# Gate products of a banded-attention and two-MLP kernel: which banks they alternate between, and what may stand before a bank's reading in the engines' lists

## The chip, the cores and the metric

The kernel runs on one core of a Trainium2 chip. The metric is device microseconds of one execution on that core. TensorE (PE) does the matmuls and has its own row for weight loads (PEld); VectorE (DVE), ScalarE (ACT) and GpSimd (POOL) do the elementwise work, and SyncE (SP) issues the DMAs.

## The reference

The part that matters, cut:

```
x = attention(q, k, v)            # 4 batches, 8 heads, 768 rows, 64 wide: 4 sinks and a window of 128 rows
a = x @ w1                        # (3072 x 512) @ (512 x 1024)
b = x @ w2
h = a * b @ w3                    # (a * b) @ w3
x = h @ w_out
h = x @ w_in                      # the second MLP
solu = h * softmax(h)
out = layernorm(solu) * g_ln @ w_out
```

All of it is fp32. The change lies in the two products a and b and in their elementwise product a * b, the gate.

## The kernel before

The kernel does its matmuls in a split form: an fp32 operand is held as a high part and a low part, each in a shortened fp32 type, and a product is three matmuls (high by high, high by low, low by high). The large products are also done by seven products on blocks of half the size in place of eight (Strassen and Winograd's scheme; `FACTORS` says which sum of blocks each of the seven takes on the left and on the right). So every operand is a sum of blocks, and each sum is made and split into parts by **operand pieces**: sums (`plus`, L368, on DVE or POOL), high parts (`acopy`, L158, on ACT) and low parts (`do_step`, L365, on DVE). New weights are first converted by L342, L351 (DVE), L359 (POOL) and L158 (ACT).

The program goes through attention, then the gate, then the product by w3 with w_out folded into it, then the second MLP. The gate, which is what the change touches, works on one batch (768 rows of x) after the other, and for each batch on four column groups m: 16 groups in all. A group has seven products k, each for two halves z (z = 0 for x @ w1, z = 1 for x @ w2). One (k, z) is six matmuls of 128x384 (`product`, which calls `mm` on L155), so there are 224 of them. They are written into PSUM, which the program holds as four tiles of two banks each: in the trace and below, bank0 is a tile with the banks X of z = 0 and Y of z = 0, bank1 has Z of z = 0 and X of z = 1, bank2 has Y of z = 1 and Z of z = 1, and bank3 has the banks 6 and 7, which the gate doesn't use before the change. Product 2 goes to X, products 5 and 3 to Z, products 1, 6, 7 and 4 to Y. Products that go to the same bank one after the other without a restart add to what stands there.

A finished bank is **read**: by an ACT copy into scratch memory (`copy`, L158, arF<-bank), or by a DVE addition of the bank to what was copied before (`two`, L948, arF<-bank,arF). Before the change a group has copies of products 1, 6, 7 and 4 and DVE readings of the others and of the bank Z at product 7; two finished halves are then multiplied on DVE (`two` with ALU.mult, arF<-arF), and the result is sent to DRAM by a DMA (`send`, L938).

What follows what on each engine isn't the order in which the code is written. Every step is put on a list of tasks (`op`) with an engine, an own estimate of its duration and a rank; `arrange` runs a small simulation of the engines over the list, in which an engine that comes free takes the task of the lowest rank among those whose inputs are ready. The instructions are then issued in that order, and each engine works through its own list strictly in order on the chip. Operand pieces of the next group or batch, conversions of new weights and readings of banks share the lists of DVE and ACT.

Of the kernel before, what the change touches and what calls it, by code (L numbers as in the profile page):

```python
# [26 lines left out]
    mask=62.62, load=22.12, scores=-355.79, max=-67.26, exp=-12.34, total=-62.48, norm=40.89, T=-21.59,  # L27
    stay=29.46, R_T=-100.61, sink_T=-182.3, T_copy=-50.24, sink_copy=-116.03, V=51.95, out=-62.87, w_load=18.71,
    w_a=-69.73, w_b=67.42, w_c=24.26, w_hi=47.52, w_lo=3.94, fold=163.21, fold_out=40.78, parts=-92.47,
    spill=-105.5, x_parts=71.86, later=-5.34, stage=0.0,  # L30
)
WO_AT, WO_BY, W3_AT, W3_BY, W12_AT, W12_BY = -4.0, 3.0, 21.0, 3.4, 30.0, 12.0
OWN_NS, OTHER_NS, PE_NS = 19, 232, 400

OVER = dict(DVE=82, ACT=95, POOL=45)

PART_OF = dict(scores="rows", V="columns")
SWITCH = {("all", "rows"): 95, ("all", "columns"): 95, ("columns", "all"): 100, ("columns", "rows"): 100}
# [10 lines left out]
def arrange(tasks, ranks=None):  # L49
# [3 lines left out]
    rank = [t[2] + ranks[t[3]] for t in tasks]  # L53
# [18 lines left out]
    free = {e: 0 for e in engine}  # L72
# [3 lines left out]
    kind = "all"  # L76
# [7 lines left out]
    while len(order) < len(tasks):  # L84
        start, eng = min(
            (free[e] if go[e] else max(free[e], wait[e][0][0]), e) for e in free if go[e] or wait[e]
        )
        while wait[eng] and wait[eng][0][0] <= start:
            n = heapq.heappop(wait[eng])[1]
            heapq.heappush(go[eng], (rank[n], n))  # L90
        n = heapq.heappop(go[eng])[1]
        change = 0
        if eng == "PE":
            heapq.heappush(go[eng], (rank[n], n))
            to = {x: PART_OF.get(tasks[x[1]][3], "all") for x in go[eng]}
            x = min(go[eng], key=lambda x: (x[0] + stay * ((kind, to[x]) in SWITCH), x[1]))
            go[eng].remove(x)
            heapq.heapify(go[eng])
            n, change, kind = x[1], SWITCH.get((kind, to[x]), 0), to[x]
        if tasks[n][0][-1] == "+" and port > start:  # L100
            others = [x for x in go[eng] if tasks[x[1]][0][-1] != "+"]
            if others:
                heapq.heappush(go[eng], (rank[n], n))
                go[eng].remove(min(others))
                heapq.heapify(go[eng])
                n = min(others)[1]
            else:
                start = port
        order.append(n)
        end = start + tasks[n][1] + change  # L110
        free[eng] = max(start, end - OVER.get(eng, 0))
        if tasks[n][0][-1] == "+":
            port = free[eng]
        for m in follow[n]:
            lag = OWN_NS if engine[m] == eng else PE_NS if eng == "PE" else OTHER_NS
            at_ns[m] = max(at_ns[m], end + tasks[n][8] + lag)
            before[m] -= 1
            if not before[m]:
                heapq.heappush(wait[engine[m]], (at_ns[m], m))
# [4 lines left out]
def attention_moe_kernel(  # L124
# [52 lines left out]
    def path(stack, banded):  # L177
# [744 lines left out]

        tasks = []

        def op(eng, ns, rank, outs, ins, f, *args, after=0, both=False, then=None):

            r = set().union(*(toks(a) for a in ins)) if ins else set()
            w = set().union(*(toks(a) for a in outs))
            if then is not None:
                r.add(then)  # L930
            tasks.append((eng + "+" * (eng == "POOL" or both), ns, rank, "stage", f, args, r - w, w, after))

        def dma(rank, out, in_, then=None):

# [5 lines left out]
        def copy(rank, out, in_, cols, eng="ACT"):  # L940
            if eng == "ACT":
                op("ACT", ns_of("ACT", cols), rank, [out], [in_], acopy, out, in_)
            else:
                op("DVE", ns_of("DVE", cols), rank, [out], [in_], lambda: DVE.tensor_copy(out=out, in_=in_))
# [26 lines left out]
        X, Y, Z = 0, 1, 2  # L971
        BANK = {1: Y, 6: Y, 7: Y, 4: Y, 2: X, 5: Z, 3: Z}

        def product(k, z, rank, ns, width, left, right):

            b = bank[3 * z + BANK[k]][:, 0:width]
            (lh, ll), (rh, rl) = left, right
            items = []
            for c in range(len(lh)):
                items += [(lh[c], rh[c]), (lh[c], rl[c]), (ll[c], rh[c])]  # L980
            op("PE", ns, rank, [b], [*lh, *ll, *rh, *rl], run, b, items, k in (1, 2, 5))
            return b

        both = [(1, 0), (1, 1), (2, 0), (6, 0), (2, 1), (6, 1), (5, 0), (7, 0), (5, 1), (7, 1), (4, 0), (3, 0), (4, 1), (3, 1)]
        when = {}
        for i, (k, z) in enumerate(both):
            when.setdefault(k, i)
# [40 lines left out]
        for bi, b in enumerate(order):  # L1028
# [4 lines left out]
            for m in range(4):  # L1033
# [33 lines left out]
                for k, z in both:  # L1067
                    l, r = FACTORS[k]
                    bk = product(
                        k, z, now, MM, TH, [[gw[z][:, l, u, c, :] for c in range(2)] for u in range(2)],  # L1070
                        [[xop[:, xlie[r], u, c, :] for c in range(2)] for u in range(2)],
                    )
                    now += MM
                    if k in (1, 6, 7):
                        copy(now, {1: p_, 6: u2, 7: u3}[k][z], bk, TH)
                    if k == 2:
                        two("DVE", now + 2000, p_[z], bk, p_[z], TH)
                        if z:
                            two("DVE", now + 5000, p_[0], p_[0], p_[1], TH, ALU.mult)
                            send(0, p_[0], now + 5000)  # L1080
                    if k == 7:
                        two("DVE", now, u3[z], bank[3 * z + Z][:, 0:TH], u3[z], TH)
                        if z:
                            two("DVE", now + 5000, u3[0], u3[0], u3[1], TH, ALU.mult)
                            send(3, u3[0], now + 5000)
# [10 lines left out]
                            send(2, u2[0], now + 5000)  # L1096


        MM = 2082
        abop = [hold[:, 12 * i * KB:12 * (i + 1) * KB].rearrange("p (u c n) -> p u c n", u=2, c=4) for i in range(3)]  # L1100
        abk = [t.rearrange("p (c n) -> p c n", c=4) for t in (
# [317 lines left out]
```

## Time and profile before

| | us |
|---|---|
| median of three runs (926.5 to 927.68) | 927.65 |
| the profiled execution, its own time | 927.59 |
| its span | 925.2 |
| PE busy, of the span | 888.6 (96%) |
| DVE busy | 700.0 (76%) |
| ACT busy | 548.8 (59%) |
| the gate, from its first matmul to the first of the next stage | 263.38 to 521.68 |

A row of the trace that lists single instructions gives the start, the duration, the engine, the line, what is written and read, how many instructions of the same kind follow one another (x), and in brackets how long the engine was idle before and what released it. "PE ... [0.74 <-DVE arF L948]" is a matmul that stood still for 0.74 us until a DVE addition on line 948 was done. Durations of one instruction include a start-up that overlaps the one before, so that the distance between starts (the pitch) can be shorter than the duration.

### The profile page before, as it was taken

The page shows a single profiled execution, that of the slowest core. Times are in us where ns is not written, and L with a number is a line of the kernel's source. Part 1 is how long each engine was busy: PE and PEld are TensorE (multiplying, and loading weights), DVE is VectorE, ACT ScalarE, POOL GpSimd, SP SyncE. Part 2 cuts the span into 40 slices and gives each one's busy share as a digit, 9 for nine tenths or more (in the row PEclk, how much of TensorE's full clock was granted, in tenths as well). Part 3 has the DMA queues.
Part 4 walks back from the last instruction along what each step waited for, and adds up shares of the span by engine and source line. Part 5 has one row for each costly group of instructions (what it writes and reads, how often), then busy time and mean ns, then how long its engine had stood idle before and what let it go on. Part 6 is the DMA issues. An engine that isn't in the chain of part 4 may idle for free.

```text
span 925.2 us, 15584 instructions
## 1 busy us (share of the span) xinstructions
PE 888.6 (96%) x5392; PEld 749.8 (81%) x5392; DVE 700.0 (76%) x1646; ACT 548.8 (59%) x1251; POOL 183.4 (20%) x243
## 2 busy tenths in 40 slices
PE   7999999999999899999998999999999999999996
PEld 3555665665579898989888999999888888999996
DVE  6988888676958786773776897794788877898761
ACT  6887877765746444752543566563667576755441
POOL 2664655451225322120000000000010011000000
PEclk9999999999999999999999999999999999999999
DMA  7566657632236367563132265443243343454411
GB/s 273 182 232 235 204 188 252 215 123 80 69 100 184 128 203 240 191 214 125 56 130 76 85 208 188 158 146 124 104 146 127 125 160 137 172 194 143 177 58 61
DMA packets 84760, 143.72 MB, mean 155 GB/s; under 512 B 6976, under 2 KB 58432, under 8 KB 82240
## 3 DMA queue, kind: packets, MB, share of 16 engines
q1 hardware_dynamic: 84672, 142.64, 46.1%
q8 instruction: 44, 0.72, 0.3%
q14 instruction: 44, 0.36, 0.1%
HBM read 95.43 MB, written 47.19 MB: 154 GB/s over the span
## 4 chain that ended last, share of the span: by engine, by line
PE 82%; DVE 12%; DMA 2%; issue 2%; ACT 1%; POOL 1%; SPq 0%; DVEq 0%; ACTq 0%; POOLq 0%
PE bank L155 56%; PE s L155 11%; PE pa L155 6%; PE pat L644 4%; DVE arF L948 3%; PE bank L1233 2%; DVE hold L365 2%; DVE g L365 2%; PE pn L656 1%; PE pn L650 1%; DVE ar L368 1%; DVE sa L600 1%; DMA arF<-in_moe_w_in_dram 1%; DVE ring L661 1%; DMA qk<-in_qk_dram 1%
## 5 line engine op out<-in xcount | busy, mean ns | idle before, releaser
L155 PE MATMUL bank<-hold,g 128*128 128x384 f32 x2016 | 360.7, 338 | 15.4 <-DVE arF L948 11.1
L155 PEld LDWEIGHTS bank<-hold,g 128*128 128x128 f32 x2016 | 349.8, 189 | 26.4 <-DVE arF L948 19.2
L155 PE MATMUL bank<-g,hold 128*128 128x512 f32 (+1 forms) x1080 | 202.2, 342 | 0.6 <-ACT ar L158 0.5
L155 PEld LDWEIGHTS bank<-g,hold 128*128 128x128 f32 x1080 | 169.2, 190 | 22.3 <-ACT ar L158 1.0
L158 ACT ACTIVATE arF<-bank 128x384 f32<-128x384 f32 (+1 forms) x160 | 80.8, 519 | 115.5 <-PE bank L155 80.5
L615 ACT ACTIVATE sa<-sa,st 128x288 f32<-128x288 f32 (+1 forms) x192 | 95.7, 501 | 20.3 <-DVE st L600 17.4
L600 DVE CUSTOM_DVE_ANT_0 sa<-s,masks 128x288 f32<-128x288 f32 (+1 forms) x192 | 76.8, 418 | 23.9 <-PE s L155 23.6
L948 DVE TENSOR_TENSOR arF<-bank,arF 128x384 f32<-128x384 f32 x96 | 53.0, 554 | 51.7 <-PE bank L155 23.4
L365 DVE TENSOR_TENSOR hold<-ar,hold 128x384 fp32r<-128x384 f32 (+2 forms) x137 | 84.6, 648 | 8.5 <-ACT hold L158 8.2
L1221 POOL TENSOR_TENSOR stt<-stt,half 128x1 f32<-128x1 f32 x24 | 17.3, 721 | 371.0 <-DVE stt L1219 363.2
L158 ACT ACTIVATE hold<-ar 128x384 fp32r<-128x384 f32 (+2 forms) x137 | 75.4, 586 | 18.0 <-DVE ar L368 13.8
L155 PE MATMUL s<-qk 64*128 64x288 f32 (+2 forms) x384 | 75.0, 439 | 8.0 <-DMA qk<-in_qk_dram 6.0
L158 ACT ACTIVATE ar<-bank 128x256 f32<-128x256 f32 (+1 forms) x80 | 33.8, 423 | 73.9 <-PE bank L155 73.5
L155 PE MATMUL bank<-g,g 128*128 128x256 f32 x504 | 66.3, 285 | 3.9 <-DVE ar L948 2.2
L661 DVE COPY ring<-pat 128x512 f32<-128x512 f32 (+1 forms) x96 | 60.9, 640 | 11.3 <-PE pat L644 10.9
L155 PEld LDWEIGHTS bank<-g,g 128*128 128x128 f32 x504 | 62.5, 192 | 5.5 <-DVE ar L948 3.0
L155 PEld LDWEIGHTS s<-qk 64*128 64x128 f32 x384 | 34.0, 193 | 35.9 <-issue 15.0
L155 PE MATMUL s<-hold 128*128 128x512 f32 x192 | 59.5, 423 | 0.0
L155 PE MATMUL pa<-ring,vn 128*64 128x256 f32 (+1 forms) x448 | 56.1, 357 | 1.5 <-DVE ring L661 1.0
L644 PE MATMUL pat<-identr,sa 128*128 128x128 f32 x352 | 56.5, 281 | 0.0
L948 DVE TENSOR_TENSOR ar<-bank,ar 128x256 f32<-128x256 f32 (+1 forms) x60 | 28.4, 475 | 32.9 <-ACT ar L158 19.1
L368 DVE TENSOR_TENSOR ar<-ar 128x256 f32<-128x256 f32 (+3 forms) x92 | 51.5, 571 | 0.8
(97 smaller groups left out, 1150.4 us busy)
## 6 DMA issues: line engine op xcount, KB each, us to landing
qk<-in_qk_dram SPq DMA_DIRECT2D x15, 1088.0 KB, 5.1
raw<-in_moe_w_dram SPq DMA_DIRECT2D x24, 512.0 KB, 5.1
abd<-arF SPq DMA_DIRECT2D x64, 192.0 KB, 2.0
lnd<-arF SPq DMA_DIRECT2D x48, 256.0 KB, 2.2
ar<-lnd SPq DMA_DIRECT2D x8, 1024.0 KB, 5.6
vn<-in_v_dram SPq DMA_DIRECT2D x16, 384.0 KB, 3.2
arF<-abd SPq DMA_DIRECT2D x8, 768.0 KB, 5.0
ar<-abd SPq DMA_DIRECT2D x8, 768.0 KB, 4.7
```

The costliest lines, as they stand in the source:

```text
L155: PE.matmul(o, lhsT=l, rhs=r, start=start, stop=stop, skip_group_check=True)
L158: ACT.activation(out=o, in_=i, func=AF.Copy, scale=s)
L365: eng.tensor_tensor(out=lo, in0=src, in1=fl(hi), op=ALU.subtract)
L368: eng.tensor_tensor(out=out, in0=a, in1=b, op=ALU.add if sign > 0 else ALU.subtract)
L600: DVE.tensor_tensor_reduce(out=sa[s][:, h, :n], in0=s_bank[s_at(s, h)][:, :n], in1=m_qb[j, h], op0=ALU.add, op1=ALU.min, scale=-scale, sca ...
L615: ACT.activation(out=a[:, h, :n], in_=a[:, h, :n], func=AF.Exp, scale=-1.0, bias=st_t[s][:, h:h + 1], accum_out=rs_t[p, j // 2][:, i:i + 1],)
L644: PE.transpose(pt[:, h, u, :], a[:, h, o:o + P], ident)
L650: PE.transpose(pn[0:n + 2 * SINKS, s % 2, :], a[:, 256 - n:256 + 2 * SINKS], ident)
L661: DVE.tensor_copy(out=ring[:, :, 2 * j + u0:2 * j + 2, :], in_=pat_t.pop(s)[:, :, u0:, :])
L948: eng, ns_of(eng, cols), rank, [out], [a, b], lambda: engines[eng].tensor_tensor(out=out, in0=a, in1=b, op=o),
L1221: op("POOL", 550, rank + 900, [st[7]], [st[6]], lambda: POOL.tensor_tensor(out=st[7], in0=st[6], in1=half, op=ALU.pow))
L1233: PE.transpose(bk[:, i * P:(i + 1) * P], e[:, (4 * g + i) * P:(4 * g + i + 1) * P], ident)
```

## The change

Four edits. The products of a group are put in the order 1, 2, 6, 5, 7, 3, 4, with both halves of each one after the other. In the odd groups (m = 1 and 3) the products that went to the banks Y go to the banks 6 and 7 of the tile bank3. Product 5 is copied by ACT in place of product 7, and DVE then adds the bank of product 7 to that copy. And `arrange` gets a rule for the gate: an operand piece on ACT or DVE (kind "gate") that would end later than 200 ns before the next reading of a bank (kind "bank") that is known to come due on that engine isn't placed; another piece that fits is taken, or the engine is left idle until the reading is due.

```
+MARGIN = 200
...
+        if tasks[n][3] == "gate" and eng in ("DVE", "ACT"):
+
+            due = min((t for t, m in wait[eng] if tasks[m][3] == "bank" and rank[m] < rank[n] + 4000), default=None)
+            if due is not None:
+                fits = [x for x in [(rank[n], n)] + sorted(go[eng]) if start + tasks[x[1]][1] - OVER[eng] + MARGIN <= due]
+                if not fits:
+                    heapq.heappush(go[eng], (rank[n], n))
+                    free[eng] = due
+                    continue
...
-            tasks.append((eng + "+" * (eng == "POOL" or both), ns, rank, "stage", f, args, r - w, w, after))
+            kind = "stage"
+            if gate_is_on[0] and eng in ("ACT", "DVE"):
+                kind = "bank" if {a.tensor.name for a in ins} & banks else "gate"
+            tasks.append((eng + "+" * (eng == "POOL" or both), ns, rank, kind, f, args, r - w, w, after))
...
-            b = bank[3 * z + BANK[k]][:, 0:width]
+            b = bank[6 + z if other and BANK[k] == Y else 3 * z + BANK[k]][:, 0:width]
...
-        both = [(1, 0), (1, 1), (2, 0), (6, 0), (2, 1), (6, 1), (5, 0), (7, 0), (5, 1), (7, 1), (4, 0), (3, 0), (4, 1), (3, 1)]
+        both = [(k, z) for k in (1, 2, 6, 5, 7, 3, 4) for z in range(2)]
...
-                        [[xop[:, xlie[r], u, c, :] for c in range(2)] for u in range(2)],
+                        [[xop[:, xlie[r], u, c, :] for c in range(2)] for u in range(2)], m % 2 == 1,
...
-                    if k in (1, 6, 7):
-                        copy(now, {1: p_, 6: u2, 7: u3}[k][z], bk, TH)
+                    if k in (1, 6, 5):
+                        copy(now, {1: p_, 6: u2, 5: u3}[k][z], bk, TH)
...
-                        two("DVE", now, u3[z], bank[3 * z + Z][:, 0:TH], u3[z], TH)
+                        two("DVE", now, u3[z], bk, u3[z], TH)
...
+        gate_is_on[0] = False
```

The lists before the gate are the same as before, and so are those from the w3 stage on. Three places show what moves in the gate; the four tiles have the numbers bank0_3009 to bank3_3012.

**PE, the last group of the gate (the fourth batch, m = 3).** Each x6 is one (k, z); x12 is two of them after each other into the same tile. hold and g23 are the operands. Before:

```order
L155 MATMUL bank0_3009<-hold_74,g23_3003 128x384 x6
L155 MATMUL bank2_3011<-hold_74,g23_3003 128x384 x6
L155 MATMUL bank0_3009<-hold_74,g23_3003 128x384 x12
L155 MATMUL bank1_3010<-hold_74,g23_3003 128x384 x6
L155 MATMUL bank2_3011<-hold_74,g23_3003 128x384 x6
L155 MATMUL bank1_3010<-hold_74,g23_3003 128x384 x6
L155 MATMUL bank0_3009<-hold_74,g23_3003 128x384 x6
L155 MATMUL bank2_3011<-hold_74,g23_3003 128x384 x12
L155 MATMUL bank0_3009<-hold_74,g23_3003 128x384 x6
L155 MATMUL bank1_3010<-hold_74,g23_3003 128x384 x6
L155 MATMUL bank2_3011<-hold_74,g23_3003 128x384 x12
```

Now:

```order
L170 MATMUL bank3_3012<-hold_74,g23_3003 128x384 x12
L170 MATMUL bank0_3009<-hold_74,g23_3003 128x384 x6
L170 MATMUL bank1_3010<-hold_74,g23_3003 128x384 x6
L170 MATMUL bank3_3012<-hold_74,g23_3003 128x384 x12
L170 MATMUL bank1_3010<-hold_74,g23_3003 128x384 x6
L170 MATMUL bank2_3011<-hold_74,g23_3003 128x384 x6
L170 MATMUL bank3_3012<-hold_74,g23_3003 128x384 x12
L170 MATMUL bank1_3010<-hold_74,g23_3003 128x384 x6
L170 MATMUL bank2_3011<-hold_74,g23_3003 128x384 x6
L170 MATMUL bank3_3012<-hold_74,g23_3003 128x384 x12
```

Before, a tile came up again after one (k, z) into another tile, or at once. Now the two halves of products 1, 6, 7 and 4 go to the two banks of one tile back to back, and two of other products lie between. In the even groups (not shown) the tiles bank0, bank2 and bank1 take turns, with one (k, z) between two that go to the same tile at six places of each group.

**DVE, the fourth batch, m = 1 and the start of m = 2.** L948 (L968 now) with a bank is a reading, with arF alone the product of two halves; L368 (L383 now) are sums and L365 (L380 now) low parts of operands, that is pieces. Before:

```order
L948 TENSOR_TENSOR arF_3004<-arF_3004,bank2_3011 128x384
L368 TENSOR_TENSOR ar1_75<-ar1_75 128x256
L365 TENSOR_TENSOR g01_73<-ar1_75,g01_73 128x256
L948 TENSOR_TENSOR arF_3004<-bank2_3011,arF_3004 128x384
L365 TENSOR_TENSOR g01_73<-ar1_75,g01_73 128x2x256
L948 TENSOR_TENSOR arF_3004<-arF_3004 128x384
L365 TENSOR_TENSOR g01_73<-ar1_75,g01_73 128x2x256
L368 TENSOR_TENSOR ar1_75<-ar1_75 128x256 x2
L948 TENSOR_TENSOR arF_3004<-bank0_3009,arF_3004 128x384
L365 TENSOR_TENSOR g01_73<-ar1_75,g01_73 128x2x256 x3
L948 TENSOR_TENSOR arF_3004<-bank1_3010,arF_3004 128x384
L368 TENSOR_TENSOR ar1_75<-ar1_75 128x256
```

Now:

```order
L968 TENSOR_TENSOR arF_3004<-bank3_3012,arF_3004 128x384
L383 TENSOR_TENSOR ar1_75<-ar1_75 128x256
L968 TENSOR_TENSOR arF_3004<-bank3_3012,arF_3004 128x384
L968 TENSOR_TENSOR arF_3004<-bank1_3010,arF_3004 128x384
L968 TENSOR_TENSOR arF_3004<-bank2_3011,arF_3004 128x384
L968 TENSOR_TENSOR arF_3004<-arF_3004 128x384 x2
L968 TENSOR_TENSOR arF_3004<-arF_3004,bank3_3012 128x384
L380 TENSOR_TENSOR g01_73<-ar1_75,g01_73 128x2x256 x4
L968 TENSOR_TENSOR arF_3004<-bank0_3009,arF_3004 128x384
L380 TENSOR_TENSOR g01_73<-ar1_75,g01_73 128x256
L968 TENSOR_TENSOR arF_3004<-bank1_3010,arF_3004 128x384
L380 TENSOR_TENSOR g01_73<-ar1_75,g01_73 128x2x256
```

Before, one to three pieces stood right ahead of most readings. Now readings stand behind readings, and the pieces are gathered behind the last reading of a group, or single between readings that are further apart.

**DVE, the first batch, the fourth group (m = 3), where the weights g23 of this group are still being made.** Before, from the reading of product 7 to the low parts:

```order
L948 TENSOR_TENSOR arF_3004<-bank2_3011,arF_3004 128x384
L948 TENSOR_TENSOR arF_3004<-bank1_3010,arF_3004 128x384
L948 TENSOR_TENSOR arF_3004<-arF_3004 128x384
L948 TENSOR_TENSOR arF_3004<-arF_3004,bank2_3011 128x384
L948 TENSOR_TENSOR arF_3004<-bank0_3009,arF_3004 128x384
L948 TENSOR_TENSOR arF_3004<-bank2_3011,arF_3004 128x384
L365 TENSOR_TENSOR g23_3003<-ar1_75,g23_3003 128x2x256
L948 TENSOR_TENSOR arF_3004<-arF_3004 128x384
L365 TENSOR_TENSOR g23_3003<-arF_3004,g23_3003 128x2x256 x2
```

Now:

```order
L968 TENSOR_TENSOR arF_3004<-bank1_3010,arF_3004 128x384
L968 TENSOR_TENSOR arF_3004<-bank2_3011,arF_3004 128x384 x2
L968 TENSOR_TENSOR arF_3004<-arF_3004 128x384
L968 TENSOR_TENSOR arF_3004<-arF_3004,bank2_3011 128x384
L968 TENSOR_TENSOR arF_3004<-arF_3004 128x384
L380 TENSOR_TENSOR g23_3003<-ar1_75,g23_3003 128x2x256 x2
L380 TENSOR_TENSOR g23_3003<-arF_3004,g23_3003 128x2x256 x2
L968 TENSOR_TENSOR arF_3004<-arF_3004 128x384
```

Before, the readings stood among the low parts. Now the readings of products 7, 3 and 4 of z = 1 and two multiplications (the second of them of the same halves) all stand ahead of four low parts; product 6 of z = 0 of the fourth group takes the second of these low parts with its third matmul.

## Rows read from the trace of the kernel before

**Rows 1.** The page: part 1 (busy us, share, instructions), one group of part 5 (mean ns).

```profile
PE 888.6 (96%) x5392; PEld 749.8 (81%) x5392; DVE 700.0 (76%) x1646; ACT 548.8 (59%) x1251; POOL 183.4 (20%) x243
...
L155 PE MATMUL bank<-hold,g 128*128 128x384 f32 x2016 | 360.7, 338 | 15.4 <-DVE arF L948 11.1
```

**Rows 2.** Windows of batches 1, 4, all: PE, PEld, DVE, ACT, POOL, PEclk, DMA, GB/s.

```profile
263.38:329.53 66.15, 62.64 (x336) 59.58 (x337) 51.04 (x85) 35.84 (x70) 25.49 (x25) 0.97 0.48 151
...
456.20:521.68 65.48, 60.40 (x338) 57.93 (x337) 47.19 (x96) 29.61 (x61) 0.00 (x0) 1.00 0.32 101
sum 258.30, PE 243.78 PEld 233.49 DVE 180.82 ACT 129.01 POOL 45.98; mean PE 60.95 PEld 58.37 DVE 45.21 ACT 32.25 POOL 11.49
```

**Rows 3.** Waits of PEld in the gate (262 to 523): total us, times, longest.

```profile
PEld bank L155 <- DVE arF L948: 19.2, 24, 1.5
PEld bank L155 <- ACT arF L158: 4.4, 6, 1.3
```

**Rows 4.** Timeline of PE behind the gate (532 to 560): one run of matmuls without a gap.

```profile
531.80 28.41 PE L155 MATMUL bank<-hold,g 128*128 128x384 f32 x163
```

**Rows 5.** Windows at the gate's start; the columns of rows 2.

```profile
263.40:265.20 1.80, 1.80 (x6) 1.80 (x7) 0.00 (x0) 0.00 (x0) 0.00 (x0) 0.58 0.37 90
265.20:267.20 2.00, 2.00 (x8) 2.00 (x8) 0.00 (x0) 0.49 (x1) 0.00 (x0) 0.52 1.00 345
```

**Rows 6.** Timeline of the fourth batch, m = 1: the DVE list of the second place above.

```profile
473.12 0.42 DVE L368 TENSOR_TENSOR ar<-ar 128x256 f32<-128x256 f32 x1
...
473.46 0.42 DVE L365 TENSOR_TENSOR g<-ar,g 128x256 fp32r<-128x256 f32 x1
...
473.79 0.55 DVE L948 TENSOR_TENSOR arF<-bank,arF 128x384 f32<-128x384 f32 x1
...
474.40 5.48 PE L155 MATMUL bank<-hold,g 128*128 128x384 f32 x30 [0.74 <-DVE arF L948]
...
478.37 1.89 DVE L365 TENSOR_TENSOR g<-ar,g 128x512 fp32r<-128x512 f32 x3
...
480.18 0.55 DVE L948 TENSOR_TENSOR arF<-bank,arF 128x384 f32<-128x384 f32 x1
...
480.78 1.66 PE L155 MATMUL bank<-hold,g 128*128 128x384 f32 x8 [0.91 <-DVE arF L948]
```

**Rows 7.** Timeline of the third batch: a DVE reading with no piece ahead of it.

```profile
414.00 4.50 PE L155 MATMUL bank<-hold,g 128*128 128x384 f32 x25
...
415.83 0.56 DVE L948 TENSOR_TENSOR arF<-bank,arF 128x384 f32<-128x384 f32 x1 [0.48 <-ACT arF L158]
```

**Rows 8.** Timeline of the first batch: an ACT reading with no piece ahead of it.

```profile
280.46 3.81 PE L155 MATMUL bank<-hold,g 128*128 128x384 f32 x21
...
281.52 0.49 ACT L158 ACTIVATE arF<-bank 128x384 f32<-128x384 f32 x1 [0.57 <-PE bank L155]
```

**Rows 9.** Groups by line and shape in the gate (263.4 to 521.8): busy us, mean ns.

```profile
L948 DVE TENSOR_TENSOR arF<-bank,arF 128x384 f32<-128x384 f32 x95 | 52.4, 554 | 51.7 <-PE bank L155 23.4 <-ACT arF L158 22.6 <-ACT hold L158 3.9
L948 DVE TENSOR_TENSOR arF<-arF 128x384 f32<-128x384 f32 x49 | 29.8, 608 | 0.7
...
L365 DVE TENSOR_TENSOR g<-ar,g 128x512 fp32r<-128x512 f32 x18 | 13.6, 776 | 1.3 <-ACT g L158 1.3
...
L158 ACT ACTIVATE arF<-bank 128x384 f32<-128x384 f32 x112 | 54.4, 488 | 99.6 <-PE bank L155 80.5 <-DVE arF L948 13.0 <-DVE arF L342 3.2
```

**Rows 10.** Timeline of the first batch, third group: a reading late behind a DMA.

```profile
302.39 0.49 ACT L158 ACTIVATE arF<-bank 128x384 f32<-128x384 f32 x1 [0.30 <-DMA abd<-arF]
...
302.93 1.38 PE L155 MATMUL bank<-hold,g 128*128 128x384 f32 x6 [0.92 <-ACT arF L158]
```

**Rows 11.** Timeline of the second batch: a conversion that waits for its load.

```profile
351.82 1.24 ACT L158 ACTIVATE arF<-arF 128x512 f32<-128x512 f32 x2 [1.72 <-DMA arF<-in_moe_w_in_dram]
...
354.70 2.38 PE L155 MATMUL bank<-hold,g 128*128 128x384 f32 x12 [0.95 <-ACT arF L158]
```

**Rows 12.** Window of 120 us right behind the gate; the columns of rows 2.

```profile
522.00:642.00 120.00, 120.00 (x688) 119.11 (x687) 97.93 (x200) 66.71 (x141) 0.00 (x0) 1.00 0.51 165
```

More of the change, by code (lines that the diff above doesn't have):

```diff
@@ L29 @@
     w_a=-69.73, w_b=67.42, w_c=24.26, w_hi=47.52, w_lo=3.94, fold=163.21, fold_out=40.78, parts=-92.47,
-    spill=-105.5, x_parts=71.86, later=-5.34, stage=0.0,
+    spill=-105.5, x_parts=71.86, gate=0.0, bank=0.0, later=-5.34, stage=0.0,
 )
@@ L99, in arrange @@
             n, change, kind = x[1], SWITCH.get((kind, to[x]), 0), to[x]
+        if tasks[n][3] == "gate" and eng in ("DVE", "ACT"):
[6 more added lines that the diff above has]
+                    continue
+                if fits[0][1] != n:
+                    heapq.heappush(go[eng], (rank[n], n))
+                    go[eng].remove(fits[0])
+                    heapq.heapify(go[eng])
+                    n = fits[0][1]
         if tasks[n][0][-1] == "+" and port > start:
@@ L923, in path @@
         tasks = []
+        gate_is_on = [True]
         def op(eng, ns, rank, outs, ins, f, *args, after=0, both=False, then=None):
@@ L972, in path, with product @@
         BANK = {1: Y, 6: Y, 7: Y, 4: Y, 2: X, 5: Z, 3: Z}
-        def product(k, z, rank, ns, width, left, right):
-            b = bank[3 * z + BANK[k]][:, 0:width]
+        def product(k, z, rank, ns, width, left, right, other=False):
+            b = bank[6 + z if other and BANK[k] == Y else 3 * z + BANK[k]][:, 0:width]
             (lh, ll), (rh, rl) = left, right
```

## The prediction

> **What bounds the kernel now.** I read the page's busy times first: PE is busy for 888.6 us of the span of 925.2 [rows 1], so the matmuls bound the kernel, and a change that leaves their number alone can win only what PE stands still. Behind the gate there is nothing of the kind to win: in the 120 us after it PE is busy for 120.00 us [rows 12]. I then cut the gate into windows. It lasts 258.30 us [rows 2]. What it would last without a stop comes from a run of 163 matmuls of the same form without a gap [rows 4]: 28.41 us less the 0.34 of one matmul [rows 1], over 162, is 0.1733 us a matmul, 1.04 us for the six of one product and half. The gate's 224 take 232.9 us, so **25.4 us are lost**. The waits of PE's weight loads in that stretch say to what: 19.2 us in 24 waits to DVE additions on line 948, 4.4 us in 6 waits to ACT copies on line 158 [rows 3], which are the readings of banks.
>
> The timeline shows how one arises. At 474.40 PE has stood for 0.74 us; the reading it waited for ran at 473.79, behind a sum at 473.12 and a low part at 473.46 [rows 6], both pieces for later products (the order of DVE's list before shows the same rows). At 480.78 it is 0.91 us, and three low parts of 1.89 us stand ahead of the reading at 480.18 [rows 6]. By the lists, the matmuls at 474.40 write bank Y of z = 1, and the reading that they waited for is of bank Z of z = 1: waits go by the tile of two banks, not by the bank. Without a piece ahead, a reading hides behind one product: DVE reads at 415.83 within a run of 25 matmuls from 414.00 that has no gap [rows 7], ACT at 281.52 within 21 [rows 8].
>
> **The sum.** I take the change by what is lost in the gate afterwards, since matmuls, readings and pieces keep their numbers and their kinds: copying product 5 and adding bank 7 in place of the reverse is one ACT copy and one DVE addition as before, cost 0. DVE is busy for 180.82 of the gate's 258.30 us and ACT for 129.01 [rows 2]; in a gate of 242 us DVE would be at 75%, so idling an engine until a reading is due has room. In the first batch DVE has 51.04 us of 66.15 [rows 2], the tightest place.
>
> *The slack of a place.* With one product between, a reading has 1.04 us; it takes 0.55 on DVE or 0.49 on ACT [rows 9], and about 0.05 on each side to be told and to tell (estimated from the gap of some 0.06 between the reading's end, 473.79 + 0.55, and 474.40). That leaves 0.40 us on DVE, 0.45 on ACT. With two between, two readings after each other fit; with three, two readings and pieces.
>
> *What goes.* In odd groups nothing is left with only one product between. In even groups six readings each have one between, all of them single, and the new rule keeps pieces from standing ahead. So the 30 waits, 23.6 us [rows 3], go, but for these terms:
>
> 1. *Start of the gate, 1.7 us, stays.* The granted clock is 0.58 and 0.52 of full over 1.80 and 2.00 us [rows 5], the lower of the clock's two levels for about half of that time; 1.80 x 0.42 + 2.00 x 0.48 = 1.7. The lists ahead of it don't change.
>
> 2. *First batch, 4.3 us, in part new.* Here the weights' parts are made while they are used. In the fourth group product 6 of z = 0 takes a low part that now stands behind two readings, two multiplications and one more low part, and all this can start only when product 4 is done. By the pitches [rows 6] (a reading 0.47 before the next, a multiplication the same, by the three low parts 0.63 each) that is 4 x 0.47 + 2 x 0.63 = 3.1; plus 0.05 and a restart of 0.1, less the two matmuls that run before (0.35), 3.0 us. Product 4 waits for a reading that itself waits for the product just ahead: 0.05 + 0.55 + 0.05 + 0.1 = 0.75. Two places in the second group have two DVE readings in the time of one product: 0.05 + 2 x 0.5 + 0.2 - 1.04, about 0.25 each, 0.5. The trace of before has such stops there as well (0.92 us at 302.93 behind a reading late by a DMA [rows 10]). Bounds: 2 us if the low parts are ready sooner than the lists say, as a plan's wait need not bind; 8 if pieces of the weights come as late as in [rows 10] at four more places.
>
> 3. *Late loads, 2.0 us, bounds 0 and 5.* The new rule goes by planned times, and a load isn't planned exactly: at 351.82 ACT waited 1.72 us for a load, and PE then 0.95 at 354.70 [rows 11]. I take two such places, at none to five.
>
> 4. *Even groups, 0.8 us.* Eight groups at 0.1 us. The rows without a gap [rows 7, 8] say 0; 3 would be every eighth of the 48 places late by 0.5, as with a low part ahead.
>
> Sum 8.8 us; gain 25.4 - 8.8 = 16.6, and 927.6 - 16.6 = **911.0 us**. The sum is made against the profiled execution, 927.59; the median, 927.65, is the same.
>
> *A rule.* The Trainium skill ("PSUM — Partial Sum Buffer", section "PSUM bank collisions raise a hardware error") wants accesses guarded by bank, and calls each bank a RAM of its own. By that rule the even groups would have three products between as well, term 4 would be 0 and 0.8 of term 2 would go: 909.4 us. The trace disagrees in what is waited for: the wait at 474.40 was for the other bank of a tile.
>
> *Further on.* The lists behind the gate are the same, and PE is dense there; what DVE or ACT bring along later from the gate (two pieces more of some 225 are left over at its end) has 22 us of idle DVE in 120 [rows 12] to hide in. Cost 0; without that cover it would be the two pieces, 1.2 us.
>
> **Rivals.**
>
> *A: half of the waits come back, 919.* The plan doesn't know waits by pairs of banks as late as they are on the chip, nor loads, so that pieces stand ahead of readings again in time though not by plan. For it: the first batch and the late load [rows 10, 11]; against it: most of DVE's readings of the new lists are followed, not preceded, by pieces. Ten waits at the mean of 19.2 / 24 = 0.8 us [rows 3] add 8: 919.0.
>
> *B: nearly nothing is lost, 906.* Term 2 at its low bound and terms 3 and 4 at 0: 1.7 + 2 = 3.7 left, 905.9. For it: readings without pieces show no gap [rows 7, 8]. Against: [rows 10].
>
> *C: slower, 930.* The even groups have 6 x 8 = 48 places with one product between. The slack is 0.40 us. One low part ahead takes 0.63 [rows 6], less the slack, plus a restart of 0.1 and some 0.07 because a lone one takes 0.69 before the next: 0.4 us a place. If it happens at all 48, that is 19.2 us over the forecast: 930.2. It decides from about 42 places up (42 x 0.4 = 16.8, all the gain). For it: a reading that must wait for its copy on the other engine is late by more than the plan. Against: each group would need a piece ahead at almost every place, and the new order shows rows of readings.
>
> *D: the change doesn't take effect in time,* as idling DVE delays operands: DVE would have to run out of its 25% idle time. Then the gain is used up by operand waits, within 0.2% of before.
>
> By the rule of the page, 909.4 lies within my forecast's own range; that waits go by single banks I hold at 3 in 100.
>
> **Chances and range.** Forecast, 907 to 916: 0.65 (the rule's 0.03 within). A, 916 to 922: 0.16. B, under 907: 0.12. D: 0.03, C: 0.04. The range takes in B's 905.9 and A's 919.0: 905.5 to 919.5. About 0.2% (1.9 us) is what a measurement of this kernel can tell from no change. Faster 0.93, same 0.03, slower 0.04.
>
> **What would show it.** In the profile of the changed kernel: a gate of about 242 us; waits of weight loads on line 968 down from 19.2 us to some 6, most of them in its first 66 us, with one of about 3 us in the fourth group; no wait at all in most odd groups; PE as dense as before behind the gate. A lower clock behind the 3 us stop would add up to the 1.7 us of term 1. I am wrong if the waits on line 968 are spread evenly over the even groups (C or A), or if weight loads wait for low parts and high parts in the later batches (D).

## The result, and the profile after

The changed kernel takes 913.9 us (median of 4 runs, 911.94 to 914.43) against 927.08 us for the kernel before (median of 4 runs beside it): a ratio of 0.9859, 95% interval [0.9835, 0.9883], or 13.1 us. The profiled execution took 911.94 us, span 909.6, which is 15.65 us less than the one of before. The forecast was 16.6 us, 911.0. So it was faster, by the mechanism that the waits were read to have, but by a fifth less than forecast. And the experiments below show that one of its parts, the order of the products, gives most of the gain by itself.

Part 1 of the page (busy us, share of the span, instructions), as in [rows 1]:

```profile
PE 881.6 (97%) x5392; PEld 750.7 (83%) x5392; DVE 697.6 (77%) x1646; ACT 546.6 (60%) x1251; POOL 185.1 (20%) x243
```

Windows of the gate's first batch, its fourth batch and the whole gate, and of 120 us behind it (columns of [rows 2]):

```profile
263.05:328.76 65.71, 60.68 (x336) 59.72 (x337) 46.68 (x82) 35.56 (x71) 25.36 (x24) 0.97 0.47 151
447.02:506.33 59.31, 59.20 (x337) 58.16 (x337) 50.14 (x103) 31.34 (x66) 2.61 (x2) 1.00 0.43 147
263.05:506.33 243.28, 237.33 (x1344) 234.36 (x1345) 177.12 (x333) 125.41 (x254) 46.81 (x40) 0.99 0.48 159
...
507.00:627.00 120.00, 120.00 (x689) 119.26 (x688) 98.50 (x201) 67.86 (x144) 0.00 (x0) 1.00 0.51 169
```

The gate went from 258.30 us [rows 2] to 243.28. Its fourth batch went from 65.48 to 59.31 and is nearly dense; its first batch, 66.15 before, has hardly moved. Behind the gate nothing changed [rows 12]. The waits of PE's weight loads in the gate (total us, times, longest), as in [rows 3]:

```profile
PEld bank L170 <- DVE arF L968: 4.3, 7, 1.8
PEld bank L170 <- DVE g L380: 3.2, 1, 3.2
PEld bank L170 <- ACT arF L173: 1.4, 2, 1.0
```

The 19.2 us in 24 waits for DVE additions became 4.3 in 7. PE's timeline over the whole gate is now five rows:

```profile
263.05 25.24 PE L170 MATMUL bank<-hold,g 128*128 128x384 f32 x144 [0.91 <-DVE ar L718]
289.77 22.17 PE L170 MATMUL bank<-hold,g 128*128 128x384 f32 x126 [1.48 <-DVE arF L968]
312.60 1.68 PE L170 MATMUL bank<-hold,g 128*128 128x384 f32 x8 [0.65 <-DVE arF L968]
317.17 84.26 PE L170 MATMUL bank<-hold,g 128*128 128x384 f32 x472 [2.89 <-DVE g L380]
402.15 113.01 PE L170 MATMUL bank<-hold,g 128*128 128x384 f32 x644 [0.72 <-ACT arF L173]
```

**The stop of 2.89 us** is the one that the forecast named: in the fourth group, product 6 waits for low parts that stand behind two readings and two multiplications. The timeline there (DVE, then PE):

```profile
313.96 0.56 DVE L968 TENSOR_TENSOR arF<-bank,arF 128x384 f32<-128x384 f32 x1 [1.42 <-PE bank L170]
...
314.43 0.55 DVE L968 TENSOR_TENSOR arF<-arF 128x384 f32<-128x384 f32 x1
...
314.90 0.55 DVE L968 TENSOR_TENSOR arF<-arF,bank 128x384 f32<-128x384 f32 x1
...
315.36 0.55 DVE L968 TENSOR_TENSOR arF<-arF 128x384 f32<-128x384 f32 x1
...
315.83 1.29 DVE L380 TENSOR_TENSOR g<-ar,g 128x512 fp32r<-128x512 f32 x2
...
317.17 4.12 PE L170 MATMUL bank<-hold,g 128*128 128x384 f32 x14 [2.89 <-DVE g L380]
```

Behind it the granted clock (third number from the end) falls to 0.50, the lower of its two levels (1.2 of 2.4 GHz), and comes back; windows of the changed kernel:

```profile
317.00:319.00 2.00, 1.83 (x6) 1.83 (x7) 2.00 (x5) 0.14 (x1) 0.00 (x0) 0.50 0.80 191
319.00:321.00 2.00, 2.00 (x10) 2.00 (x9) 2.00 (x5) 0.71 (x2) 0.00 (x0) 0.68 0.83 326
321.00:324.00 3.00, 3.00 (x19) 3.00 (x18) 1.54 (x4) 1.90 (x5) 0.00 (x0) 1.00 0.77 303
```

That is 2.00 x 0.50 + 2.00 x 0.32 = 1.6 us more.

**The two other stops**, 1.48 us at 289.77 and 0.72 at 402.15, have a DMA at their root. The first (ACT, DVE, PE in the timeline):

```profile
288.64 0.49 ACT L173 ACTIVATE arF<-bank 128x384 f32<-128x384 f32 x1 [1.90 <-DMA abd<-arF]
...
289.16 0.56 DVE L968 TENSOR_TENSOR arF<-bank,arF 128x384 f32<-128x384 f32 x1 [2.41 <-ACT arF L173]
...
289.77 1.48 PE L170 MATMUL bank<-hold,g 128*128 128x384 f32 x7 [1.48 <-DVE arF L968]
```

An ACT copy of a bank waits because the buffer that it writes is still being sent to DRAM for the group before. The DVE reading behind the copy is late, and so is the product. The second, in the ninth group (ACT, then PE), where the product waits for the late copy itself:

```profile
401.61 0.49 ACT L173 ACTIVATE arF<-bank 128x384 f32<-128x384 f32 x1 [3.13 <-DMA abd<-arF]
...
402.15 1.66 PE L170 MATMUL bank<-hold,g 128*128 128x384 f32 x8 [0.72 <-ACT arF L173]
```

### The profile page after: what moved, and what is told of

It reads as the page before. It is cut to its first block, busy times and chain, and to the rows that moved or that the text cites. A ratio compares the mean times of both kernels' runs of the same rounds, so it can differ in the third digit from the quotient of the medians.

```text
span 909.6 us, 15582 instructions
## 1 busy us (share of the span) xinstructions
PE 881.6 (97%) x5392; PEld 750.7 (83%) x5392; DVE 697.6 (77%) x1646; ACT 546.6 (60%) x1251; POOL 185.1 (20%) x243
## 4 chain that ended last, share of the span: by engine, by line
PE 88%; DVE 7%; DMA 2%; ACT 1%; issue 1%; SPq 0%; POOL 0%; DVEq 0%; ACTq 0%
PE bank L170 63%; PE s L170 11%; PE pa L170 6%; PE pat L659 4%; PE bank L1254 2%; PE pn L671 1%; PE pn L665 1%; DVE sa L615 1%; DVE hold L380 1%; DMA abd<-arF 1%; DVE ring L676 1%; DVE arF L968 1%; DMA qk<-in_qk_dram 1%; DVE g L380 1%; DVE ar L383 1%
## 5 line engine op out<-in xcount | busy, mean ns | idle before, releaser
L170 PE MATMUL bank<-hold,g 128*128 128x384 f32 x2016 | 354.0, 336 | 6.9 <-DVE g L380 2.9
L968 DVE TENSOR_TENSOR arF<-bank,arF 128x384 f32<-128x384 f32 x96 | 52.4, 555 | 53.8 <-PE bank L170 30.9
L380 DVE TENSOR_TENSOR hold<-ar,hold 128x384 fp32r<-128x384 f32 (+2 forms) x137 | 85.7, 654 | 7.0 <-ACT hold L173 6.6
L1242 POOL TENSOR_TENSOR stt<-stt,half 128x1 f32<-128x1 f32 x24 | 18.2, 757 | 311.0 <-DVE stt L1240 303.1
L676 DVE COPY ring<-pat 128x512 f32<-128x512 f32 (+1 forms) x96 | 60.9, 639 | 11.5 <-PE pat L659 11.1
L968 DVE TENSOR_TENSOR ar<-bank,ar 128x256 f32<-128x256 f32 (+1 forms) x60 | 28.5, 476 | 32.3 <-ACT ar L173 18.5
L173 ACT ACTIVATE hold<-arF 128x384 fp32r<-128x384 f32 (+2 forms) x82 | 42.4, 554 | 16.5 <-DVE arF L383 5.3
```

Of the source, the lines that this page charges most:

```text
L170: PE.matmul(o, lhsT=l, rhs=r, start=start, stop=stop, skip_group_check=True)
L173: ACT.activation(out=o, in_=i, func=AF.Copy, scale=s)
L380: eng.tensor_tensor(out=lo, in0=src, in1=fl(hi), op=ALU.subtract)
L676: DVE.tensor_copy(out=ring[:, :, 2 * j + u0:2 * j + 2, :], in_=pat_t.pop(s)[:, :, u0:, :])
L968: eng, ns_of(eng, cols), rank, [out], [a, b], lambda: engines[eng].tensor_tensor(out=out, in0=a, in1=b, op=o),
L1242: op("POOL", 550, rank + 900, [st[7]], [st[6]], lambda: POOL.tensor_tensor(out=st[7], in0=st[6], in1=half, op=ALU.pow))
```

## The experiments

For all kernels one number is taken in the same way from the profile: the time from the gate's first matmul to the first of the next stage, and what of it is above 1.041 us for each product and half, the time that the kernel itself plans for one (with the forecast's 232.9 us for all 224, the losses of a gate would be 0.3 us larger). "First batch" counts the first 56 of these, "later" the other 168. Each row of these three columns is one execution. The medians carry, beside this, what happens ahead of the gate, which none of the kernels changes but where the profiles differ (last section).

| kernel | order | third banks | rule | gate us | lost, first batch | lost, later | median us | ratio to before |
|---|---|---|---|---|---|---|---|---|
| before (profile shown) | old | no | no | 258.3 | 7.9 | 17.3 | 927.08 | |
| before, once more | old | no | no | 256.4 | 6.8 | 16.4 | | |
| banks only | old | yes | no | 252.3 | 6.0 | 13.1 | 920.33 | 0.9938 [0.9916, 0.996] |
| rule only | old | no | yes | 248.0 | 3.2 | 11.6 | 917.79 | 0.9912 [0.9888, 0.9935] |
| order only | new | no | no | 244.2 | 4.7 | 6.3 | 909.36 | 0.9815 [0.9797, 0.9832] |
| order and rule | new | no | yes | 243.1 | 3.0 | 6.9 | 911.99 | 0.984 [0.9822, 0.9858] |
| order and banks | new | yes | no | 242.3 | 4.2 | 4.9 | 911.07 | 0.9836 [0.9818, 0.9853] |
| the change | new | yes | yes | 243.3 | 7.4 | 2.7 | 913.9 | 0.9859 [0.9835, 0.9883] |
| the change, once more | new | yes | yes | 243.6 | 7.4 | 3.0 | 913.19 | 0.9848 [0.9828, 0.9868] |

The kernels stood beside different runs of before (medians 925.78 to 927.08), so the ratios are what is compared, and differences under some 0.3% are inside their intervals. "Order" takes in the copy of product 5 in place of product 7; the two were not tried apart.

**The two kernels once more.** The changed kernel:

> The changed kernel once more, beside the others. If the first profile is typical: a gate of 243 to 245 us, one stop of 2.9 us in the fourth group with the lower clock behind it (some 1.6 us), two stops of 0.7 to 1.5 us behind a send that is late, and 911 to 912 us. If that profile was a lucky one: 913.5 to 914.5 us, with the lower clock at the gate's start as well, as in the kernel before (1.7 us).

It took 913.19 us (5 runs, 910.86 to 914.15). The gate was the same as in the first profile, 243.6 us, with the same three stops, so that profile is typical in the gate. Neither case came as it was put: the median is near the second, but the lower clock at the gate's start, which the second went by, is not there. The 2 us between the two profiled executions (911.94 and 913.86) lie ahead of it: the gate began at 263.05 and at 265.09. The kernel before:

> The kernel before once more, for a second profile. If the lower clock at the gate's start (1.7 us) belongs to that kernel, the gate lasts 258 us again. If it was an accident of the one execution, the granted clock there is 1.00 and the gate lasts 256.3 to 257 us, so that the change is worth 13 us there and not 15.

Windows of this second profile, the whole gate and its start:

```profile
265.00:521.38 256.38, 242.00 (x1344) 231.90 (x1345) 180.88 (x334) 128.83 (x257) 46.05 (x40) 1.00 0.47 153
265.00:267.00 2.00, 2.00 (x11) 2.00 (x12) 0.00 (x0) 0.49 (x1) 0.00 (x0) 1.00 0.44 106
```

It took 927.39 us (one run). The granted clock at the start is 1.00 here, against 0.58 and 0.52 in [rows 5]; the gate is 1.9 us shorter than in the profile that the forecast was made from, and begins 1.6 us later. 256.4 less 243.3 is 13.1 us, which is the measured gain.

**The rule left out.** The edits that follow are against the changed kernel.

```
-        if tasks[n][3] == "gate" and eng in ("DVE", "ACT"):
+        if False:
```

> The new order and the third pair of banks, without the rule that keeps pieces from standing ahead of readings. Theory 1 (the rule is needed: pieces ahead cost the time): at the 48 places of the even groups with one product between, pieces stand ahead again, 0.4 us each at a third to a half of them: 6 to 10 us slower than with the rule, 918 to 923 us. Theory 2 (the order and the banks alone give the slack): within 2 us of the changed kernel, and perhaps faster by up to 3 us, because the stop of 2.9 us in the fourth group goes.

911.07 us, 0.9836: theory 2. Without the rule the later batches lose 2 us more (4.9 for 2.7 to 3.0), and the first one 3 us less: its fourth group, where the stop of 2.9 us was, loses 0.1 us for 5.5, but its third 3.3 for 0.1.

**The rule alone**, old order and banks:

```
-        both = [(k, z) for k in (1, 2, 6, 5, 7, 3, 4) for z in range(2)]
+        both = [(1, 0), (1, 1), (2, 0), (6, 0), (2, 1), (6, 1), (5, 0), (7, 0), (5, 1), (7, 1), (4, 0), (3, 0), (4, 1), (3, 1)]
...
-                        [[xop[:, xlie[r], u, c, :] for c in range(2)] for u in range(2)], m % 2 == 1,
+                        [[xop[:, xlie[r], u, c, :] for c in range(2)] for u in range(2)], False,
...
-                    if k in (1, 6, 5):
-                        copy(now, {1: p_, 6: u2, 5: u3}[k][z], bk, TH)
+                    if k in (1, 6, 7):
+                        copy(now, {1: p_, 6: u2, 7: u3}[k][z], bk, TH)
...
-                        two("DVE", now, u3[z], bk, u3[z], TH)
+                        two("DVE", now, u3[z], bank[3 * z + Z][:, 0:TH], u3[z], TH)
```

> The kernel before with the rule alone: old order, old banks, product 7 copied. Theory 1 (the rule carries the gain): the readings are free of pieces, two-thirds of the 23.6 us of waits go, some 912 to 916 us. Theory 2 (without slack the rule cannot win): 924 to 930 us, waits on the DVE additions still 15 us or more, since two readings behind each other don't fit into one product, pieces or not.

917.79 us: between the two. The waits of weight loads in the gate:

```profile
PEld bank L170 <- DVE arF L968: 10.8, 15, 1.0
PEld bank L170 <- ACT arF L173: 2.5, 4, 1.3
```

So the rule is worth something by itself, some 8 us of the gate (256.4 less 248.0), but 10.8 us of waits on DVE additions stay with it in force.

**The third pair of banks left out** (`m % 2 == 1` becomes `False`):

> The change with the third pair of banks left out: all 16 groups as the even ones are now, one product between at six places of each. If a single reading behind one product hides as the rows without a gap say: 1 to 3 us slower than the changed kernel, with waits of some 0.2 to 0.6 us in odd groups. If one product between is too tight in practice (slack 0.40 us): 8 odd groups lose as much as 1.5 us each, 10 to 14 us slower, no better than the kernel before.

911.99 us, the same as the change, where even the milder of the two cases had it 1 to 3 us slower. One product between is enough at most places where one reading stands there, as the rows without a gap had said [rows 7, 8], but not at all: in the later batches leaving the banks out costs 4 us (6.9 for 2.7 to 3.0), most of it in the odd groups (4.4 for 0.8). In the first batch it saves 4, in the fourth group.

**The order alone**, without the rule (`if False:`) and without the third banks (`False`):

> The order of products alone (with product 5 copied, which goes with it), without the rule and without the third pair of banks. Theory 1 (the order carries nearly all of it, and rule and banks take away the same waits once more): 910 to 914 us, a gate of 242 to 244 us. Theory 2 (the order needs one of the two others to have its slack): 917 to 921 us, a gate of 248 us or more, with waits spread over the later groups.

909.36 us: theory 1, a little under its range. The waits of weight loads on DVE additions fell from 19.2 us to 5.3, though the copies on ACT now cost more than the 4.4 us of before [rows 3]:

```profile
PEld bank L170 <- ACT arF L173: 6.1, 10, 1.7
PEld bank L170 <- DVE arF L968: 5.3, 12, 1.5
```

In this kernel the rule isn't there, and pieces do stand ahead of readings. Its timeline in the fourth batch (DVE and PE):

```profile
449.70 1.02 DVE L380 TENSOR_TENSOR hold<-ar,hold 128x384 fp32r<-128x384 f32 x2
449.82 12.50 PE L170 MATMUL bank<-hold,g 128*128 128x384 f32 x71
...
450.63 0.55 DVE L968 TENSOR_TENSOR arF<-bank,arF 128x384 f32<-128x384 f32 x1
...
451.10 1.02 DVE L380 TENSOR_TENSOR hold<-ar,hold 128x384 fp32r<-128x384 f32 x2
...
452.04 0.55 DVE L968 TENSOR_TENSOR arF<-bank,arF 128x384 f32<-128x384 f32 x1
```

Two readings, each right behind two low parts, within a run of 71 matmuls that has no gap. Counted over the gate in the traces, by what ran on DVE less than 0.1 us before a reading; in brackets how many of these readings a weight load of PE then waited for, and how long in all:

| ahead of the DVE reading | before | order alone | the change |
|---|---|---|---|
| a piece or a conversion of weights | 37 (16, 13.8 us) | 39 (9, 3.2 us) | 35 (3, 0.8 us) |
| a reading or a multiplication | 15 (8, 5.4 us) | 19 (3, 2.0 us) | 14 (2, 0.8 us) |
| nothing, DVE was idle | 58 (0) | 53 (0) | 62 (2, 2.8 us) |

In the kernel before, no reading that found DVE idle made PE wait. Readings behind pieces are as many after the change as before it: they weren't removed, they ceased to matter, for the most part by the order alone.

**The banks alone**, old order, no rule:

> The kernel before with the third pair of banks in its odd groups alone: old order, no rule, product 7 copied. If any distance between a reading and the next write into its tile does it: the odd groups (half of the 23.2 us lost) win as with the new order, some 6 to 8 us, 918 to 920 us. If it is the order that keeps two readings, or a reading and its pieces, out of the time of one product: a wait moves from the DVE additions to the copies on ACT, which now stand behind pieces, and less than 4 us are won, 922 to 927 us.

920.33 us, between the two again. The waits:

```profile
PEld bank L170 <- ACT arF L173: 11.1, 19, 1.4
PEld bank L170 <- DVE arF L968: 7.4, 10, 1.2
```

4.4 us in 6 waits for ACT copies [rows 3] became 11.1 in 19: the wait moved to the other engine, as the second case had it, though 4 us of the gate were won.

**The rule from the second batch on:**

```
-            if gate_is_on[0] and eng in ("ACT", "DVE"):
+            if gate_is_on[0] and now >= 56 * 1041 - 1 and eng in ("ACT", "DVE"):
```

> The changed kernel with the rule from the second batch on only. If the rule is what makes the stop of 2.9 us in the fourth group: that stop and the low clock behind it go, the first batch loses some 4 us as it does without the rule (4.2), the later ones 2.7 as they do with it: a gate of 240 us, 909 to 911 us. If the weights' parts are late there anyway: 243 us and 912 to 914 us as with the rule.

907.35 us, 0.9805 [0.9784, 0.9825]; gate 239.5 us, 4.2 lost in the first batch and 2.2 later. Both as expected, and the median is below the expected 909 to 911: with the rule out of the first batch the stop of 2.9 us isn't there, nor the lower clock behind it. The rule is not enough to make that stop, though: with it in force the fourth group loses 1.5 us without the third banks, and nothing with the buffer that follows.

**One buffer more:**

```
-        arF = lp2.tile([P, int(26.5 * KB)], F32, name="arF")
+        arF = lp2.tile([P, int(28 * KB)], F32, name="arF")
...
-        tmp = [atF(1.5 * i, 1.5) for i in range(7)]
+        tmp = [atF(1.5 * i, 1.5) for i in range(7)] + [atF(26.5, 1.5)]
...
-                p_, u2, u3, cc = tmp[0:2], tmp[2:4], tmp[4:6], tmp[6]
+                three, g = [tmp[0], tmp[2], tmp[7]], 4 * bi + m
+                p_, u2, u3, cc = [three[2 * g % 3], tmp[1]], [three[(2 * g + 1) % 3], tmp[3]], tmp[4:6], tmp[6]
```

> The changed kernel with one buffer more: the results of products 2 and 3 take turns on three buffers, so that a copy doesn't have to wait for the send of the group before. If the two stops in the second and ninth group (1.5 to 1.7 and 0.9 to 1.3 us) come from a send that is late behind larger loads: both go, 2.5 to 2.9 us faster than the changed kernel. If a late load or a late piece is behind the send: less than 1 us.

910.8 us, 0.9821 [0.9802, 0.984]; gate 239.7 us. The stops of the second and the ninth group are gone (each of these groups loses under 0.05 us now), 3.7 us in all with the first batch. There the fourth group loses nothing now, but the third 4.1 us, with a wait for a low part again:

```profile
PEld bank L170 <- DVE g L380: 1.8, 1, 1.8
```

**Combinations.** Both repairs:

> Both repairs of the changed kernel: the rule from the second batch on, and the third buffer for products 2 and 3. Each alone left 6.4 and 6.5 us lost in the gate. If they mend different places: the late send in the third batch stays as with each alone (0.7), the first batch keeps some 3.3 to 4 us: 5.5 to 6.5 us lost, no better than either. If the third group's stop (3.3 to 4.1 us in both) came from the late sends: 3 us lost, 904 to 906 us.

908.93 us, 0.9817 [0.9791, 0.9843], gate 239.5 us, 6.3 lost: no better than either, as expected. The order and the buffer without rule and banks:

> The new order with the third buffer, without the rule and without the third pair of banks. If order and buffers are what matters: 5 to 7 us lost in the gate, 906 to 909 us, as good as with the rule and the banks. If rule or banks are needed for the last few us: 9 to 11 us lost as with the order alone, 909 to 911 us.

913.46 us, 0.9862 [0.9839, 0.9885], 11.4 us lost, of which 1.7 at the start by the lower clock. A miss: the buffer won little there (9.7 us lost without the start, against 11.0 with the order alone), and with the buffer rule and banks are worth 3 us of the gate (6.3 lost with both repairs). The median is 4 us above that of the order alone, most of which the gate doesn't show; the mean granted clock of its five runs is 0.991 to 0.995, that of the order alone 0.998 to 0.999. And both repairs with another layout of the banks:

```
-            b = bank[6 + z if other and BANK[k] == Y else 3 * z + BANK[k]][:, 0:width]
+            b = bank[2 * BANK[k] + z if gate_is_on[0] and not (other and BANK[k] == Y) else 6 + z if other and BANK[k] == Y else 3 * z + BANK[k]][:, 0:width]
```

> Both repairs, and the banks laid out so that in every group the two halves of one product share a tile (X with X, Y with Y, Z with Z). If waits by pairs of banks cost the even groups their slack: their remaining losses (0.35, 0.17 and the like, some 1 us in all outside the first batch) go, and the first batch's stop between readings of the two halves with it, 1 to 4 us faster than without this layout. If the pairs don't matter: the same within 1 us.

906.0 us (904.58 to 907.38), 0.9773 [0.9751, 0.9795]: the lowest median of all, 20.6 us less than before, though its interval overlaps with that of the rule from the second batch on. The timeline of PE over the gate and the windows at its start:

```profile
263.66 144.83 PE L170 MATMUL bank<-hold,g 128*128 128x384 f32 x816 [0.91 <-DVE ar L718]
409.00 46.05 PE L170 MATMUL bank<-hold,g 128*128 128x384 f32 x264 [0.51 <-DVE arF L968]
455.95 54.32 PE L170 MATMUL bank<-hold,g 128*128 128x384 f32 x310 [0.89 <-DVE arF L968]
```

```profile
263.66:265.40 1.74, 1.74 (x6) 1.74 (x7) 0.00 (x0) 0.00 (x0) 0.00 (x0) 0.57 0.27 62
265.40:267.40 2.00, 2.00 (x8) 2.00 (x7) 0.00 (x0) 0.00 (x0) 0.00 (x0) 0.52 1.04 357
```

The gate is 238.5 us. The first batch is free of stops (2.3 us lost, 1.7 of them by the lower clock at the start). The later batches lost 3.0, not less than the 2.2 without this layout, and their even groups 1.9 for 0.6: so the win is in the first batch, and this layout doesn't take away the even groups' last losses. Which of the first batch's waits this layout takes away wasn't tried apart.

## Why the prediction was right, and where its sum was off

Right were the place and the cover. The whole change of time is in the gate (15.0 of the 15.65 us between the two profiles), no term came up behind it, and the waits on DVE additions fell to 4.3 us as forecast (some 6, most in the first batch; the one of 3 us that these took in is the 3.2 for low parts). The measured 913.9 lies in the forecast's range. The sum of what would be left was too small: 8.8 us, where the profile has 10.1 (243.28 less 224 x 1.041) and the second one 10.4. And without the term for the start, which is not in these profiles, it is 7.1 against 10.0 to 10.3. These 3 us are nearly all of the 3.5 between the forecast's gain and the measured one.

- **"Start of the gate, 1.7 us, stays" was wrong, and cancels.** The lower clock at the start was taken for a property of the kernel and left on both sides. It is in neither profile of the changed kernel (0.1 us lost in the first group), nor in the second of the kernel before. It comes and goes, and happened to lie in the one execution that the sum was made against. As it is on neither side of a typical pair, the gain of 16.6 doesn't depend on it. But that the first profile, 911.94, came within 1 us of the forecast's 911.0 is luck: the start's 1.7 us, which fell away by chance, hid over half of the 3 us. The forecast also misread the clock: with the lower level at 0.50, a mean of 0.58 and 0.52 is the lower level for nearly all of the time and not for about half of it; its 1.7 us doesn't use that.
- **"First batch, 4.3 us" was 5.5 to 5.7**, all in the fourth group. The stop of 3.0 us was 2.89, the wait of product 4 0.65 for 0.75. But the clock's fall behind the stop, 1.6 us, was only named as something that could be added, and wasn't in the sum. It should have been: the same profile showed what a start at the lower level costs [rows 5]. The two places in the second group (0.5 us) did not show.
- **"Late loads, 2.0 us" was 3.0 to 3.3**, the losses of the second and the ninth group, two places as taken, but by sends that hold a buffer and not by loads: with one buffer more both are gone.
- **"Even groups, 0.8 us" was 0.6** outside the ninth group, and the odd ones lost 0.8 from the second batch on where 0 was forecast. The Trainium skill ("PSUM — Partial Sum Buffer", "PSUM bank collisions raise a hardware error") says to guard by bank. The forecast took from this that the term would be 0 if waits went by bank; no run here guards by bank, so none bears it out. The last layout, which gives the even groups two products between, as in the odd ones, still left some 2 us in them.

The argument for the gain was right in one part and wrong in another. It was right that one product hides one reading and that a reading with pieces ahead or a second reading is late: in the kernel before, all 19.2 us of waits were for readings behind pieces, conversions, readings or multiplications. It gave the credit for removing this to the rule and the third banks ("the new rule keeps pieces from standing ahead"). The runs show otherwise: 35 DVE readings stand right behind pieces or conversions with the change, for 37 before. And of the 16.4 us lost in the later batches, the order alone takes 10.1, the rule alone 4.8, the banks alone 3.3, and all three 13.4 to 13.7, less than the 18.2 of the three alone: in part they take away the same waits. That the order does it by giving readings with pieces ahead room to be late is shown by the run of 71 matmuls and by the count of readings. Rival A was right that readings would be late against the plan, but at two places, behind sends, and not at ten. Rival C's price was never paid: with no rule at all, the pieces ahead of readings cost 2 us in the later batches.

That the order alone has a lower median than the whole change (0.3% less) goes with the clock. Its five runs, 908.77 to 911.29 us, have a mean granted clock of 0.998 to 0.999; the nine of the change have 911.16 and 910.86 at 0.997, and 911.94 to 914.43 at 0.990 to 0.994. So at like clocks the two are about the same, and medians this near to each other don't rank the kernels. Why the clocks differ stays open, and so does which of the order and the copy of product 5 counts. The losses of the order alone may be too high by some 2 us, as its profiled execution, 911.29, is the slowest of the five.

## What to carry to other kernels

Where a matmul waits for a buffer's reading, first look at how many other products lie between the reading and the next write, and how many readings must fit there: an order that leaves one reading per product does more than keeping other work off the engine, and makes that mostly needless. What a scheduler's rule is worth depends on the parts beside it and is to be measured with and without them: in the first batch this one takes 3.6 us off the losses with the old order (6.8 to 3.2) and 1.7 with the new one (4.7 to 3.0), and adds 3.2 with the new order and the third banks (4.2 to 7.4). And take a second profile of the kernel before, before a term like a low clock is booked as its own, and compare medians a few us apart only with the granted clocks of their runs beside them.

## What the runs showed of the hardware that was not expected

- The granted clock is not the same from one execution to the next at the same place. At the gate's start, with the same 0.91 us of idle time ahead of the first matmul, it was at the lower level in 3 of 14 profiles and at 1.00 in the others. Ahead of the gate, with lists that are the same in every kernel here, the gate's start lies between 262.10 and 266.52 us. The windows of the first 30 us and the next 30 us have a clock of 0.95 and 0.94 in the changed kernel and 1.00 and 1.00 in the run with the order alone, whose gate started first of all. The whole time goes with it, by some 3 us: two runs of the changed kernel with a mean granted clock of 0.997 took 911.16 and 910.86 us, three at 0.990 took 913.19 to 914.15 in the same set.
- A send of 192 KB landed in a median of 2.0 us over the whole kernel before, and in 4.5 us in the stretch of 280 to 290 us of the changed kernel, where two loads of 512 KB were issued in the 2.5 us ahead of it; ACT waited 1.90 us for that send.
